# The opening of a fused attention and expert kernel, written as some 680 jobs of one engine each

## The chip, the cores and the metric

The kernel runs on one core of a Trainium2 chip. The metric is device time in microseconds (us) of one execution. The engines are PE (matrix products, with PEld for its weight loads), DVE (vector), ACT (scalar functions), POOL (GpSimd) and SP (which here only issues transfers). A row of PE that is one pass of a matrix product is called a matmul below.

## What is computed

```python
rel = pos[:, None] - pos[None, :]
mask = (rel >= 0) & (rel < 64)
scores = np.where(mask, scale * q @ k.T, -1e9)     # batch 8, heads 8, 576 tokens, 64 wide
attn = softmax(scores) @ v
x = attn.transpose(0, 2, 1, 3).reshape(4608, 512)
xn = x / rms(x) * rms_g
g = xn @ w_gate                                    # 512 x 1536
out = (g * sigmoid(g) * (xn @ w_val)) @ w_out      # 1536 x 512
```

So it is attention over a sliding window of 64 keys, a normalisation of each token's 512 numbers, and an expert network of three weight matrices.

## The kernel before

**Precision.** Each product of the expert network is made of 16-bit halves: an operand is a high and a low f16 part, and `three` (L1008) adds high*high, high*low and low*high, so a line L1009, L1010 and L1011 stand for one product. The weights come in a wide format and are first turned into such halves on the chip. For one chunk (256 of the 1536 hidden columns, gate or val) that is: a transfer of 1 MB by `stage` (L222), two exponentials on ACT and two pairs of `pw` matmuls on PE with a DVE operation behind each (`widen_powers`, `widen_rest`), a maximum on DVE, a common scale (`in_scale`: one small matmul and a few small DVE and POOL operations), and the split (L261 to L269): high half on ACT, low half on DVE or POOL.

**Stages.** The opening, up to 230 us, works on three things at once:
- Attention of batches 0 and 1, four pairs of heads each. A pair has two groups. A group is `scores` (64x64 matmuls of line L433 into two PSUM banks, one for each head of the pair), masks on DVE (L446), exponentials on ACT (L449), the sums' reciprocals on DVE, a scaling on POOL (L533), transposes on PE (`tr`, L548), copies by DVE and ACT (L551), the products with the values on PE (`xp`, L597) and a copy into `xb`. After four pairs come the sums of squares: `tot` on PE (L852), eleven small DVE operations for the inverse roots (L868 to L875), a broadcast on PE (`rb`, L921), and the normalised token halves `xn` on DVE, ACT and POOL (L950 to L959).
- The preparation of the six chunks of gate and val, and of the six of `w_out`.
- The first tile of 512 tokens: for each of 12 blocks of 128 hidden columns the matmuls `pg` and `pv` (12 each), tanh on ACT, two DVE operations, the hidden halves; then `po`, four token blocks of 36 matmuls each. The second tile has its first two chunks (EARLY = 2) here too.

Tile 1's third chunk (`pg_1_4`) and all that comes behind it is called the tail below. There the remaining batches, tiles and weights are woven into one written order.

**What sets the order.** In the tail, each instruction is tied to the one written ahead of it on its engine ("written order", at the end of the program). In the opening the program only emits its parts in an order: hand-set numbers (`CFG['X']`, `['DW']`, `['DO']`, `S1`, `SC0`, `N0` and others) say at which half step of the expert work (`tick`, `advance`) which part is emitted, `behind` adds hints, and a scheduler that models the engines then chooses the order of each queue. `scores` emits its matmuls with the heads taking turns:

```python
QUARTERS = ((0, 0), (1, 1), (0, 1), (1, 0))      # head, half of the bank's rows
for i in range(2):
    for h, par in QUARTERS:
        quarter(sc[h][par * D : (par + 1) * D, i, :], qt, kk, h, 4 * g + 2 * i + 1 + par)
```

The banks of PSUM in the opening are: three `mo` (products of the expert network, and the scores of batch 0), two `xp` (also `pw`), and one each of `sc`, `tr` and `mi`. The scores of batch 1 take `sc` for one head and `mi` for the other; `mi` also serves `n2`, `tot` and `rb`.

Of the kernel before, what the change touches and what calls it, by code (L numbers as in the profile page):

```python
CFG = {'X': {'p00': 6.0, 'b00': 8.44, 't00': 9.52, 'p01': 8.44, 'b01': 10.94, 't01': 10.94, 'r': 2, 'z0': 11.94, 's00': 15.12, 's01': 12.94, 'p10': 18.61, 'd10': 8, 'd11': 13.94}, 'DW': {'d10': -6, 'p10': -4, 'b10': -12, 't10': -4, 'd11': -4, 'p11': -2.0, 'b11': -2, 't11': -1.98, 'z1': 2, 's10': 2.1, 's11': 2.05, 'd20': -2, 'p20': 0, 'b20': 0.01, 't20': 0.02, 'd21': 0, 'p21': 2, 'b21': 2, 't21': 2.02, 'z2': 6, 's20': 6, 's21': 6.05, 'd30': 2, 'p30': 2.0, 'b30': 4, 't30': 4.02, 'd31': 4, 'p31': 6, 'b31': 6.01, 't31': 8, 'z3': 10, 's30': 10.1, 's31': 11.96, 'd40': 6, 'p40': 7, 'b40': 8, 't40': 8.02, 'd41': 5.69, 'p41': 10, 'b41': 10.01, 't41': 12, 'z4': 14, 's40': 14.1, 's41': 14, 'd50': 10, 'p50': 12, 'b50': 12, 't50': 12.02, 'd51': 12, 'p51': 13.49, 'b51': 14, 't51': 14, 'z5': 15.0, 's50': 18, 's51': 18, 'D0': 17, 'W0': 19, 'D1': 18.66, 'W1': 21.59, 'D2': 19.5, 'W2': 21.5, 'D3': 20.5, 'W3': 22, 'D4': 21.5, 'W4': 22.5, 'D5': 22, 'W5': 23.5, 'O': 24.5}, 'LO': '0000100010101000', 'ADD': 'ppvppp', 'ONP': '000001110101', 'ONO': '000000', 'FB': 1, 'NB0': 0, 'HIE': 'aaaaavaaaaaa', 'HOE': 'aaaaaa', 'HHE': 'aavaaaaavaaaaaaaavavaaaa', 'XHE': 'aavvvaaaaavvaava', 'XBE': 'aaaaavaaaaaavaaa', 'X2E': 'aaaaavaa', 'DO': 'q0 k0 q1 v0 k1 q2 k2 v1 q3 k3 v2 s0 v3 s1'}

# [24 lines left out]
P = 128  # L27
# [15 lines left out]
LT0 = [1.62, 1.62, 1.62, 1.62, 1.76, 1.62, 1.76, 1.62]  # L43
LV0 = [2.6, 2.6, 2.6, 2.6, 2.6, 2.6, 2.6, 2.6]
# [37 lines left out]
def tile_window_attention_moe(  # L82
# [10 lines left out]
    nc = tc.nc  # L93

    cp = ctx.enter_context(tc.tile_pool(name="cp", bufs=1))
    wk = ctx.enter_context(tc.tile_pool(name="wk", bufs=2))
    early = ExitStack()
    ps_sc = early.enter_context(tc.tile_pool(name="ps_sc", bufs=1, space=PSUM))
    ps_tr = early.enter_context(tc.tile_pool(name="ps_tr", bufs=1, space=PSUM))
    ps_x = early.enter_context(tc.tile_pool(name="ps_x", bufs=2, space=PSUM))  # L100
    ps_mi = early.enter_context(tc.tile_pool(name="ps_mi", bufs=1, space=PSUM))
    ps_mo = early.enter_context(tc.tile_pool(name="ps_mo", bufs=3, space=PSUM))
# [15 lines left out]
    pt_pool = early.enter_context(tc.tile_pool(name="pt", bufs=NPT))  # L118
# [71 lines left out]

    def exp_bits(dst, src):
        nc.vector.tensor_scalar(dst, src.bitcast(I32), 23, None, ALU.logical_shift_right)
# [11 lines left out]
    def rms_weights():  # L204

        nc.sync.dma_start(out=gsb, in_=rms_g)
        nc.vector.tensor_reduce(gmx[:, 0:1], gsb, AX.X, ALU.max, apply_absolute_value=True)
        gps = ps_mi.tile([P, TT], F32, tag="mi", name="gps")
        nc.tensor.transpose(gps[0:1, 0:P], gmx[:, 0:1], ident)
        nc.vector.tensor_reduce(gmx[0:1, 1:2], gps[0:1, 0:P], AX.X, ALU.max)  # L210
        nc.vector.tensor_tensor(gmx[0:1, 1:2], gmx[0:1, 1:2], floor[0:1, :], ALU.max)
        gpb = ps_mi.tile([P, TT], F32, tag="mi", name="gpb")
        nc.tensor.matmul(gpb[:, 0:1], lhsT=one[0:1, :].to_broadcast([1, P]), rhs=gmx[0:1, 1:2], start=True, stop=True)
        exp_bits(gex[:, 0:1], gpb[:, 0:1])
        nc.vector.tensor_scalar(gex[:, 1:2], gex[:, 0:1], 1.0, None, ALU.add)
        nc.vector.tensor_scalar(gex[:, 2:3], gex[:, 0:1], -1.0, 253.0, ALU.mult, ALU.add)
        pow2(gpw, gex[:, 1:3])
        nc.vector.tensor_scalar(gsb, gsb, gpw[:, 1:2], None, ALU.mult)
        nc.vector.tensor_scalar(gsb_late, gsb, -0.1875, None, ALU.mult)


# [9 lines left out]
    def widen_powers(st, name):  # L231

        n = 1024
        by = st.bitcast(U8)
        top = by[:, 8 : 8 + 8 * n].rearrange("p (i e) -> p i e", e=8)[:, :, 0]
        mp = wk.tile([P, n], BF16, tag="t2k", name=f"mp_{name}", bufs=T2K)
        mn = wk.tile([P, n], BF16, tag="t2k", name=f"mn_{name}", bufs=T2K)
        nc.scalar.activation(mp, top.bitcast(I8), AF.Exp, bias=ebias[:, 0:1], scale=LN2_16)
        nc.scalar.activation(mn, top, AF.Exp, bias=ebias[:, 1:2], scale=LN2_16)
        return mp, mn  # L240

    def widen_rest(st, dst, mp, mn, name):

        for i in range(2):
            cols = slice(i * TT, (i + 1) * TT)
            pw = x_bank(f"pw_{name}_{i}")
            nc.tensor.matmul(pw, lhsT=unit[:, 0, :], rhs=mp[:, cols], start=True, stop=False)
            nc.tensor.matmul(pw, lhsT=unit[:, 1, :], rhs=mn[:, cols], start=False, stop=True)
            rest = st[:, 1 + 2 * i * TT : 1 + 2 * (i + 1) * TT].rearrange("p (i e) -> p i e", e=2)[:, :, 0]
            nc.vector.scalar_tensor_tensor(  # L250
                dst[:, cols].bitcast(I32), rest, 5, pw.bitcast(I32), ALU.logical_shift_right, ALU.bitwise_or
            )

    def widen(st, dst, name):
        mp, mn = widen_powers(st, name)
        widen_rest(st, dst, mp, mn, name)
        return mp

    def split(src, sc, hi, lo, on_pool, hv):
        if on_pool:  # L260
            nc.vector.tensor_scalar(src, src, sc, None, ALU.mult)  # L261
            (nc.vector.tensor_copy if hv else nc.scalar.copy)(hi, src)
            nc.gpsimd.tensor_tensor(lo, src, hi, ALU.subtract)
            return
        if hv:
            nc.vector.tensor_scalar(hi, src, sc, None, ALU.mult)
        else:
            nc.scalar.activation(hi, src, AF.Copy, scale=sc)
        nc.vector.scalar_tensor_tensor(lo, src, sc, hi, ALU.mult, ALU.subtract)  # L269

    def in_stage(c, i):
        w = (w_gate, w_val)[i]
        return stage(w[:, c * WC : (c + 1) * WC], NKD, f"{i}_{c}")

    tops = {}
    staged = {}
# [41 lines left out]
    def out_stage(c):  # L318
        return stage(w_out[c * WC : (c + 1) * WC, :], 2, f"o_{c}")
# [218 lines left out]
    def weights_to_keys(n, g, ps):  # L538
        pts = []
        for h in range(2):  # L540
# [11 lines left out]
            if g == h == 0:  # L552
                cpy(pt[0:D, 2, :], tr[0:D, 2, :])
# [1084 lines left out]
```

## Time and profile before

| | before |
|---|---|
| median of 3 runs | 962.68 us |
| lowest, highest | 959.09, 964.14 us |
| profiled execution | 962.36 us |
| its span | 960.6 us |
| PE busy | 934.6 us, 97% |
| DVE, ACT, POOL busy | 72%, 58%, 43% |
| mean granted clock of TensorE | 0.988 |

The span goes from the first to the last instruction of the profiled execution; 1.76 us lie around it. A row of the timeline gives start, duration, engine, line, operation, tiles, shape and count, and in brackets the idle time ahead of it with what ended it. Durations of merged rows reach from the first start to the last end; matmuls overlap, so a row of matmuls in a stream costs less than its duration says: the 512-column matmul is shown with 0.38 us and the next starts 0.21 to 0.22 us later.

### The profile page before, as it was taken

To read this page: it belongs to the slowest core of one execution; us is meant where nothing else is said; L and a number is where in the kernel's file an instruction comes from. 1 tells how busy PE (TensorE), PEld (TensorE's weight loads), DVE (VectorE), ACT (ScalarE), POOL (GpSimd) and SP (SyncE) were. 2 spreads that over 40 slices of the span, in tenths; PEclk is the share of its full clock that TensorE was granted. 3 is DMA by queue.
4 is the path that set the end of the run, shared out by engine and by line. 5 is a ranking of instruction groups with operands and counts; after the bars stand their busy time and mean duration, and the time that the engine had idled before them with its cause. 6 is when DMAs were issued, how large, how long until landed. Compare 5 with 4: busy or idle time off the path is not lost.

```text
span 960.6 us, 22333 instructions
## 1 busy us (share of the span) xinstructions
PE 934.6 (97%) x8350; PEld 683.6 (71%) x8363; DVE 689.0 (72%) x1868; ACT 558.4 (58%) x1434; POOL 413.4 (43%) x477
## 2 busy tenths in 40 slices
PE   7889999999999999999999999999999999999998
PEld 5654554444444444477888888888888888888887
DVE  5679675763778676989977887888788876733770
ACT  6658677743435553657666756775676545533552
POOL 3335562241515362445734563555454544430540
PEclk9979999899999999999999999999999999999999
DMA  8555453052736766489749974987497646555641
GB/s 306 164 158 173 139 184 132 13 158 68 177 91 175 220 194 202 147 255 319 226 179 302 315 244 154 321 281 254 154 316 265 204 144 223 172 175 196 212 154 45
DMA packets 102812, 187.59 MB, mean 195 GB/s; under 512 B 27440, under 2 KB 64304, under 8 KB 102704
## 3 DMA queue, kind: packets, MB, share of 16 engines
q1 hardware_dynamic: 102128, 184.98, 60.0%
q8 instruction: 66, 1.08, 0.5%
q10 hardware_dynamic: 576, 1.18, 0.3%
q14 instruction: 42, 0.34, 0.1%
HBM read 148.38 MB, written 37.75 MB: 194 GB/s over the span
## 4 chain that ended last, share of the span: by engine, by line
PE 86%; DVE 8%; ACT 2%; issue 2%; DMA 1%; POOL 1%; SPq 0%; DVEq 0%; ACTq 0%; POOLq 0%
PE a L1262 30%; PE o L1205 17%; PE sc L433 4%; PE pg L1009 3%; PE pg L1010 3%; PE pv L1009 3%; PE pg L1011 3%; PE pv L1011 3%; PE pv L1010 3%; PE x L571 3%; PE po L1009 2%; PE po L1011 2%; PE po L1010 2%; PE xp L597 1%; PE tr L548 1%
## 5 line engine op out<-in xcount | busy, mean ns | idle before, releaser
L1262 PEld LDWEIGHTS <-wt 128*128 128x128 f16 x3024 | 294.0, 98 | 39.1 <-issue 3.5
L1262 PE MATMUL a<-xn,wt 128*128 128x256 f16 x1728 | 203.9, 273 | 2.3 <-DVE th L1292 2.0
L1331 POOL TENSOR_TENSOR wt<-u,wt 128x512 f16<-128x512 f32 x72 | 65.8, 914 | 169.1 <-ACT wt L1329 111.8
L1262 PE MATMUL a<-wt,wt 128*128 128x256 f16 x1044 | 126.4, 273 | 0.0
L1296 ACT ACTIVATE th<-a,hsc 128x256 f32<-128x256 f32 x144 | 68.1, 473 | 99.3 <-DVE a L1360 85.3
L1331 POOL TENSOR_TENSOR h<-th,h 128x512 f16<-128x512 f32 x72 | 84.1, 1170 | 48.9 <-ACT h L1329 48.5
L1205 PE MATMUL o<-wt,h 128*128 128x256 f16 x864 | 100.4, 273 | 0.0
L1205 PEld LDWEIGHTS <-h 128*128 128x128 f16 x864 | 84.1, 98 | 10.7 <-issue 1.0
L449 ACT ACTIVATE pm<-pm,st 128x128 f32<-128x128 f32 (+1 forms) x216 | 83.9, 390 | 10.5 <-DVE st L446 9.6
L1360 DVE TENSOR_TENSOR a<-a,s 128x512 f32<-128x512 f32 x72 | 50.0, 695 | 48.2 <-PE a L1262 45.7
L404 POOL TENSOR_TENSOR pm<-pm,st 128x512 f32<-128x512 f32 (+1 forms) x72 | 63.0, 901 | 30.9 <-DMA kv<-kv 22.5
L1291 DVE SCALAR_TENSOR_TENSOR th<-th,a 128x256 f32<-128x256 f32 x144 | 59.6, 414 | 20.4 <-ACT th L1296 18.5
L1062 POOL TENSOR_TENSOR h<-th,h 128x512 f16<-128x512 f32 x30 | 36.7, 1224 | 80.4 <-ACT h L1061 68.4
L1205 PEld LDWEIGHTS <-wt 128*128 128x128 f16 x648 | 63.4, 98 | 8.9 <-issue 1.4
L433 PE MATMUL sc<-kv,q 64*64 64x128 f32 (+1 forms) x1056 | 60.3, 299 | 9.2 <-DMA q<-q 4.8
L1292 DVE SCALAR_TENSOR_TENSOR th<-a,th 128x256 f32<-128x256 f32 x144 | 61.1, 424 | 4.9
L433 PEld LDWEIGHTS sc<-kv,q 64*64 64x64 f32 x1056 | 46.0, 147 | 20.8 <-issue 6.3
L1009 PE MATMUL pg<-xn,wt 128*128 128x512 f16 x144 | 55.8, 387 | 1.1 <-ACT ot L1456 0.8
L1009 PE MATMUL pv<-xn,wt 128*128 128x512 f16 x144 | 55.4, 385 | 0.3 <-issue 0.2
L1010 PE MATMUL pg<-xn,wt 128*128 128x512 f16 x144 | 55.3, 384 | 0.1
L1010 PE MATMUL pv<-xn,wt 128*128 128x512 f16 x144 | 54.9, 381 | 0.1
L1011 PE MATMUL pv<-xn,wt 128*128 128x512 f16 x144 | 54.9, 381 | 0.1
(218 smaller groups left out, 1938.6 us busy)
## 6 DMA issues: line engine op xcount, KB each, us to landing
wt<-sevens SPq DMA_DIRECT2D x72, 512.0 KB, 5.2
wt<-sevens SPq DMA_DIRECT2D x36, 768.0 KB, 5.2
wt<-outer SPq DMA_DIRECT2D x24, 768.0 KB, 5.8
kv<-kv SPq DMA_DIRECT2D x28, 608.0 KB, 5.5
via<-pm SPq DMA_DIRECT2D x96, 144.0 KB, 3.3
pm<-via SPq DMA_DIRECT2D x24, 576.0 KB, 4.6
q<-q SPq DMA_DIRECT2D x28, 288.0 KB, 3.9
st<-w_gate SPq DMA_DIRECT2D x6, 1024.0 KB, 5.5
```

The lines of the kernel that those rows point to most:

```text
L404: nc.gpsimd.tensor_tensor(p[:, :ks, us, :], p[:, :ks, us, :], r, ALU.mult)
L433: nc.tensor.matmul(out.rearrange("p (n c) -> p n c", c=D), lhsT=qt[hd, j * D : (j + 1) * D], rhs=halves[hd, :1, :] if j == 0 else halves[h ...
L449: nc.scalar.activation(part, part, AF.Exp, bias=low, scale=-1.0, accum_out=total)
L1009: nc.tensor.matmul(acc, lhsT=lh, rhs=rh, start=first, stop=False)
L1010: nc.tensor.matmul(acc, lhsT=lh, rhs=rl, start=False, stop=False)
L1011: nc.tensor.matmul(acc, lhsT=ll, rhs=rh, start=False, stop=last)
L1205: nc.tensor.matmul(acc[:, sub * HT : (sub + 1) * HT], lhsT=l[:, x, sub * P : (sub + 1) * P], rhs=r[:, y, :], start=first and c == cs[0] an ...
L1262: nc.tensor.matmul(acc[:, i * HT : (i + 1) * HT], lhsT=ws[l][:, kt, :], rhs=b[:, m, kt, :], start=at_start, stop=kt == 1 and j == 2, skip_ ...
L1291: nc.vector.scalar_tensor_tensor(cols, cols, 1.0, acc[:, :HT], ALU.add, ALU.mult)
L1292: nc.vector.scalar_tensor_tensor(cols, acc[:, HT:], 2.0**-42, cols, ALU.mult, ALU.mult)
L1296: nc.scalar.activation(cols, acc[:, :HT], AF.Tanh, scale=th_scale[:, c : c + 1])
L1331: nc.gpsimd.tensor_tensor(lo, src, hi, ALU.subtract)
```

## The change

The functions that emitted parts of the opening (`scores`, `weights_to_keys`, `attention_events`, `first_batch`, `widen_rest`, `in_scale`, `expert_in`, `expert_out`, `tick`, `advance`, `behind` and others) give way to functions that declare jobs. A job has a name, a part that issues instructions of one engine, the jobs that it needs, and the buffers that it takes, each with the job that gives it back. `run_jobs` calls the parts in the order of a table of numbers, `ORDER`; a job whose needs are not met lets a later one by that stands at most `AHEAD` behind it. The place of `mark`, from which instructions are tied into written order on all five queues, moves ahead of the first job.

```diff
+ORDER = {'g0': 7.16, 'g1': 1.88, 'g2': 11.07, ..., 's41': 60.66, 'm410': 185.07, ..., 'V1': 200.24}
+AHEAD = 3.0
+IDLES = 0
+NUDGE = {}
...
+    def run_jobs(steps):
+        late = max(ORDER.values(), default=0)
...
+        def next_of(left):
+            limit = ORDER.get(left[0], late) + AHEAD
+            for n in left:
+                if ORDER.get(n, late) > limit:
+                    break
+                if not needs(n):
+                    return n
+            return first_of(left[0], set()) or next(n for n in left if not needs(n))
...
-    def scores(n, g, qk):
+    def group_jobs(n, g, box, norm):
...
+        tags = [("mo", f"m{k}1"), ("mo", f"m{k}1")] if n < NPAIR else [("sc", f"m{k}1"), ("mi", f"m{k}1")]
+        job(f"s{k}", score, f"q{n}", f"k{n}", takes=tags)
         for h in range(2):
+            job(f"m{k}{h}", partial(mask, h), f"s{k}", *([f"m{k}0"] if h else []),
+                takes=[] if h else [("st", f"w{k}1"), ("t2k", f"t{k}0"), ("t2k", f"t{k}1")])
+            job(f"a{k}{h}", partial(power, h), f"m{k}{h}")
+            job(f"w{k}{h}", partial(scaled, h), f"i{k}")
+            job(f"t{k}{h}", partial(turned, h), f"w{k}{h}", takes=[("sc" if n < NPAIR and h else "tr", f"u{k}{h}")])
...
-    def expert_in(t, c):
+    def expert_jobs(t, c):
...
+            for m in range(2):
+                job(f"G{k}{m}", partial(products, i, m), f"l{c}{m}", *xs, *([f"G{t}{c}00"] if i or m else ["v61"] if t else []),
+                    takes=where + [("mo", f"{'MN'[m]}{k}")])
...
-    rest = first_batch()
-    rest(1)
...
     mark = traced[-1]
+    rms_jobs()
+    for b in range(TB):
+        batch_jobs(b)
+    for c in range(NC):
+        in_jobs(c)
+    out_jobs()
+    idle_jobs(IDLES)
+    for t, cs in ((0, NC), (1, EARLY)):
+        for c in range(cs):
+            expert_jobs(t, c)
+    out_tile_jobs(0)
+    run_jobs([f"G{t}{c}{i}{m}" for t, cs in ((0, NC), (1, EARLY)) for c in range(cs) for i in range(2) for m in range(2)]
+             + [f"U{k}{half}" for k in range(TT // P) for half in range(2)])
     rest_of_tiles()
```

The instructions are the same ones but for a square of batch 1 (128x576), which moves from DVE to ACT. From `pg_1_4` on, the queues hold what they held. So the change is in the order of the opening on all queues. Three places of PE's queue show it. The names are tile names with the pair of heads or the tile first; a count behind a row is that of equal rows on end.

The first place is a score group of batch 1 (pair 6, group 0; the third number of the name is the head). Before, a head's five matmuls stand together, and the other head's come some 80 rows later:

```order
L433 MATMUL sc_6_0_0_1133<-kv_6_766,q_6_764 64x128 x4
L433 MATMUL sc_6_0_0_1133<-kv_6_766,q_6_764 64x64
L433 MATMUL sc_6_0_1_1134<-kv_6_766,q_6_764 64x128 x4
L433 MATMUL sc_6_0_1_1134<-kv_6_766,q_6_764 64x64
```

Now:

```order
L549 MATMUL sc_6_0_0_994<-kv_6_735,q_6_688 64x128
L549 MATMUL sc_6_0_1_995<-kv_6_735,q_6_688 64x128
L549 MATMUL sc_6_0_0_994<-kv_6_735,q_6_688 64x128
L549 MATMUL sc_6_0_1_995<-kv_6_735,q_6_688 64x128
L549 MATMUL sc_6_0_0_994<-kv_6_735,q_6_688 64x128
L549 MATMUL sc_6_0_1_995<-kv_6_735,q_6_688 64x128
L549 MATMUL sc_6_0_0_994<-kv_6_735,q_6_688 64x128
L549 MATMUL sc_6_0_1_995<-kv_6_735,q_6_688 64x128
L549 MATMUL sc_6_0_0_994<-kv_6_735,q_6_688 64x64
L549 MATMUL sc_6_0_1_995<-kv_6_735,q_6_688 64x64
```

The heads take turns, as the program emits them, and the group is one block. So it is in all 19 groups of pairs 0 to 10 in the change; before, in the very first and in pair 10.

The second place is that from the sums of batch 0 to the first expert product (`pw_0_1` and `pw_1_1` belong to chunk 1 of gate and of val). Before:

```order
L852 MATMUL tot_0_639<-one_94,ssq_0_296 128x1 x5
L921 MATMUL rb_0_0_660<-ident_86,rm_0_645 128x128 x4
L433 MATMUL sc_4_0_0_703<-kv_4_691,q_4_689 64x128 x4
L433 MATMUL sc_4_0_0_703<-kv_4_691,q_4_689 64x64
L1009 MATMUL pg_0_0_824<-xn_0_659,wt0_81 128x512
L1009 MATMUL pv_0_0_837<-xn_0_659,wt0_81 128x512
```

Now, with every second row of like ones left out:

```order
L979 MATMUL tot_0_646<-one_94,ssq_0_474 128x1 x5
L1051 MATMUL rb_0_0_666<-ident_86,rm_0_652 128x128 x4
L350 MATMUL pw_0_1_0_677<-mp_0_1_673,unit_91 128x512
L350 MATMUL pw_0_1_0_677<-mn_0_1_675,unit_91 128x512
L350 MATMUL pw_0_1_1_680<-mp_0_1_673,unit_91 128x512
L350 MATMUL pw_0_1_1_680<-mn_0_1_675,unit_91 128x512
L549 MATMUL sc_4_0_0_694<-kv_4_357,q_4_538 64x128
L549 MATMUL sc_4_0_1_695<-kv_4_357,q_4_538 64x128
L350 MATMUL pw_1_1_1_711<-mp_1_1_686,unit_91 128x512
L350 MATMUL pw_1_1_1_711<-mn_1_1_708,unit_91 128x512
L549 MATMUL sc_4_1_1_750<-kv_4_357,q_4_538 64x128
L1162 MATMUL pg_0_0_767<-xn_0_665,wt0_81 128x512
```

Eight `pw` matmuls and both groups of pair 4 have moved ahead of the first product; behind it, `pg_0_0` has its twelve matmuls on end where they were mixed with `pv_0_0` and `pg_0_1`. On DVE the two low halves of chunk 0 now both stand between the roots and the four operations of L1075 (L950 before), which are followed by the bits of `pw_0_1`, one cast of `xn` and the six masks of `sc_4_0`.

The third place is around the broadcast of batch 1, between tile 0 and tile 1. Before, from the last matmul of tile 0's hidden blocks on, one row of each kind:

```order
L1011 MATMUL pv_0_11_1866<-xn_0_659,wt2_83 128x512
L433 MATMUL sc_8_1_1929<-kv_8_1634,q_8_1632 64x128 x6
L921 MATMUL rb_1_0_1773<-ident_86,rm_1_1715 128x128 x3
L921 MATMUL rb_1_0_1773<-ident_86,rm_1_1715 128x64
L433 MATMUL sc_9_0_2034<-kv_9_1758,q_9_1824 64x128 x8
L433 MATMUL sc_9_1_2035<-kv_9_1758,q_9_1824 64x128 x8
L1009 MATMUL pg_1_0_1914<-xn_1_749,wt0_81 128x512
```

Now, the same way:

```order
L1164 MATMUL pg_0_10_1720<-xn_0_665,wt2_83 128x512
L979 MATMUL tot_1_1741<-one_94,ssq_1_1103 128x1 x5
L1164 MATMUL pv_0_11_1770<-xn_0_665,wt2_83 128x512
L1051 MATMUL rb_1_0_1788<-ident_86,rm_1_1747 128x128 x3
L1051 MATMUL rb_1_0_1788<-ident_86,rm_1_1747 128x64
L1162 MATMUL pv_0_10_1808<-xn_0_665,wt2_83 128x512
L1164 MATMUL pv_0_10_1808<-xn_0_665,wt2_83 128x512
L1162 MATMUL pg_1_0_1873<-xn_1_802,wt0_81 128x512
```

The blocks `pv_0_11` (the rest of it), `pv_0_10` and `pg_0_11` have moved to either side of the broadcast, and pairs 8 and 9 from ahead of `pg_1_0` to behind it.

## Rows read from the trace of the kernel before

**Rows 1.** The page: busy time of each engine, and the chain that ended last.
```profile
PE 934.6 (97%) x8350; PEld 683.6 (71%) x8363; DVE 689.0 (72%) x1868; ACT 558.4 (58%) x1434; POOL 413.4 (43%) x477
...
PE 86%; DVE 8%; ACT 2%; issue 2%; DMA 1%; POOL 1%; SPq 0%; DVEq 0%; ACTq 0%; POOLq 0%
```

**Rows 2.** Timeline of PE, where tile 0 ends and tile 1 goes on.
```profile
228.97 0.38 PE L1011 MATMUL po<-wt,h 128*128 128x512 f16 x1
230.13 0.38 PE L1009 MATMUL pg<-xn,wt 128*128 128x512 f16 x1 [0.78 <-ACT ot L1456]
```

**Rows 3.** Windows of 50 us: length, busy us (instructions) of each engine, PEclk, DMA share, GB/s.
```profile
0.00:50.00 50.00, 40.20 (x345) 29.74 (x347) 29.86 (x149) 30.33 (x99) 18.29 (x39) 0.98 0.69 238
50.00:100.00 50.00, 45.60 (x294) 24.79 (x300) 42.56 (x133) 35.40 (x82) 21.19 (x30) 0.89 0.52 162
100.00:150.00 50.00, 49.79 (x364) 26.72 (x365) 33.10 (x82) 37.56 (x69) 29.41 (x31) 1.00 0.42 141
```

**Rows 4.** What PE waited for up to 230 us: us in total, times, longest.
```profile
PE sc L433 <- DVE st L446: 3.6, 4, 2.1
```

**Rows 5.** Timeline of PE: score groups of batches 0 and 1.
```profile
4.85 2.18 PE L433 MATMUL sc<-kv,q 64*64 64x128 f32 x28 [4.85 <-DMA q<-q]
...
35.04 1.12 PE L433 MATMUL sc<-kv,q 64*64 64x128 f32 x8
...
67.73 0.76 PE L433 MATMUL sc<-kv,q 64*64 64x128 f32 x10
```

**Rows 6.** Timeline of PE: a score group of a later batch, and what follows it.
```profile
235.40 0.27 PE L433 MATMUL s<-kv,q 64*64 64x64 f32 x2
...
236.35 1.24 PE L571 MATMUL x<-pm,kv 64*64 64x128 f32 x36
```

**Rows 7.** Windows of the score line L433 alone, columns as in rows 3.
```profile
0.00:48.00 48.00, 15.63 (x144) 1.00 0.68 235
48.00:150.00 102.00, 13.07 (x160) 0.94 0.48 154
150.00:172.00 22.00, 5.64 (x48) 0.89 0.43 144
```

**Rows 8.** Timeline of PE: the same two transposes on either side of 40 us.
```profile
36.09 0.69 PE L548 MATMUL tr<-ident,p 128*128 128x128 f32 x2
...
42.37 0.44 PE L548 MATMUL tr<-ident,p 128*128 128x128 f32 x2
```

**Rows 9.** Timeline of PE: from the sums of batch 0 to the first expert product.
```profile
47.24 2.06 PE L852 MATMUL tot<-one,ssq 128*128 128x1 f32 x10 [1.41 <-DVE ssq L719]
51.68 2.04 PE L921 MATMUL rb<-ident,rm 128*128 128x128 f32 x8 [2.38 <-DVE rm L875]
...
55.22 0.58 PE L1009 MATMUL pg<-xn,wt 128*128 128x512 f16 x1 [0.23 <-ACT xn L957]
```

**Rows 10.** Timeline of DVE behind the roots of batch 0.
```profile
51.45 1.28 DVE L269 SCALAR_TENSOR_TENSOR wt<-wt,ws 128x1024 f16<-128x1024 f32 x1
53.76 2.72 DVE L950 SCALAR_TENSOR_TENSOR xb<-xb,gsb,rb 128x512 f32<-128x512 f32 x4 [1.04 <-PE rb L921]
56.40 1.74 DVE L957 CAST xn<-xb 128x512 f16<-128x512 f32 x2
```

**Rows 11.** Line L446, the masks, up to 230 us: ns min/median/max.
```profile
L446 DVE DVE_READ_ACCUMULATOR2_ANT st<- x107: 73/82/85, 7.4 to 213.7; 128x1 f32 x91, 64x1 f32 x16
L446 DVE CUSTOM_DVE_ANT_0 p<-sc,blocked x80: 209/285/293, 7.2 to 121.4; 128x128 f32<-128x128 f32 x64, 64x64 f32<-64x64 f32 x16
```

**Rows 12.** Timeline of PE: from the last product of tile 0 to the first of tile 1.
```profile
159.95 0.38 PE L1011 MATMUL pv<-xn,wt 128*128 128x512 f16 x1
...
166.93 1.94 PE L433 MATMUL sc<-kv,q 64*64 64x128 f32 x16 [2.11 <-DVE st L446]
...
171.67 0.61 PE L1009 MATMUL pg<-xn,wt 128*128 128x512 f16 x1
```

**Rows 13.** Line L269, the low halves, up to 230 us: ns min/median/max.
```profile
L269 DVE SCALAR_TENSOR_TENSOR wt<-wt,hsc x3: 1277/2082/2205, 184.5 to 194.7; 128x1024 f16<-128x1024 f32 x3
```

More of the change, by code (lines that the diff above doesn't have):

```diff
@@ L189, in tile_window_attention_moe, with job, idle_jobs, idle @@
     out_scale = hsc[:, 4, 0:1]
+    jobs = {}
+    def job(name, part, *after, takes=()):
+        assert name not in jobs, name
+        jobs[name] = part, list(after), list(takes)
+    SIZES = {"t2k": T2K, "st8": NST, "pt": NPT, "st": 3, "mo": 3, "sc": 1, "tr": 1, "mi": 1, "xp": 2, "kv": NKV, "q": NQ, "f4k": F4K,
+             "xn": 2, "xb": 1, "ssq": 1, "top": 2, "n2": 2, "z": 2, "ws": 2, "rm": 1, "mo1": 1}
+    spare = {}
+    def idle_jobs(count):
+        def idle(k):
+            if k == 0:
+                spare["to"] = ps_tr.tile([P, TT], F32, tag="tr", name="idle")
+            nc.tensor.matmul(spare["to"][:, 3 * P :], lhsT=ones, rhs=ones, start=True, stop=True, skip_group_check=True)
+        for k in range(count):
+            job(f"Y{k}", partial(idle, k), *(["Y0"] if k else []), takes=[] if k else [("tr", None)])
@@ L229, in stage, with widen_jobs @@
         return st
-    def widen_powers(st, name):
+    def widen_jobs(name, tiles, load, dst, free):
+        box = {}
         n = 1024
[L234 to L240, printed above, removed]
@@ new lines, in product, with rest @@
+        def product(j):
+            dst()
+            box["pw", j] = ps_x.tile([P, TT], F32, tag="xp", name=f"pw_{tiles}_{j}")
+            for i in range(2):
+                nc.tensor.matmul(box["pw", j], lhsT=unit[:, i, :], rhs=box[i][:, j * TT : (j + 1) * TT], start=i == 0, stop=i == 1)
+        def rest(j):
+            bits = box["st"][:, 1 + 2 * j * TT : 1 + 2 * (j + 1) * TT].rearrange("p (i e) -> p i e", e=2)[:, :, 0]
+            nc.vector.scalar_tensor_tensor(
+                dst()[:, j * TT : (j + 1) * TT].bitcast(I32), bits, 5, box["pw", j].bitcast(I32), ALU.logical_shift_right, ALU.bitwise_or
+            )
@@ new lines, in begin @@
+        def begin():
+            box["st"] = load()
+        job(f"d{name}", begin, takes=[("st8", f"r{name}1")])
+        for i in range(2):
+            job(f"e{name}{i}", partial(power, i), f"d{name}", takes=[("t2k", f"f{name}" if free and i == 0 else f"p{name}1")])
+        for j in range(2):
+            job(f"p{name}{j}", partial(product, j), f"e{name}0", f"e{name}1", takes=[("xp", f"r{name}{j}")])
+            job(f"r{name}{j}", partial(rest, j), f"p{name}{j}")
+        if free:
+            job(f"f{name}", lambda: free(box[0]), f"r{name}0", f"r{name}1")
@@ L512, in scores @@
             for i, u in enumerate(units(g, h)):
                 part[u] = p[:, i, :]
[L514 to L518 removed]
+                low = own["st"][:, 0, u - u0 : u - u0 + 1]
                 if u:
@@ L721, in roots @@
-        def roots():
-            assert chain["add", b] == NPAIR
-            norm["r"] = inverse_roots(b, norm["ssq"])
+                else:
+                    nc.gpsimd.tensor_tensor(ssq, ssq, pairs[hp][0], ALU.add)
         def wide_parts(piece):
             return wide_roots(b, norm["ssq"], pairs[NPAIR - 1][0], piece)
-        def normal(piece):
-            for part in normalise(b, norm["x"], norm["r"], piece):
-                part()
         def normal_parts(piece):
-            return normalise(b, norm["x"], norm.get("r"), piece)
```

781 lines of the change are left out of this document (410 added, 371 removed).

## The prediction

> **What bounds the kernel now.** I read the page first: PE is busy for 97% of the span and makes up 86% of the chain that ended last; no other engine is over 72% [rows 1]. So what counts is when PE gets through its queue. From `pg_1_4` on all queues hold the same rows in the same order, so the change can only move the moment at which that tail begins: 230.13 us, 1.16 us after the last `po` matmul [rows 2]. I take the tail as rigid: a microsecond won ahead of it is one won at the end. Work and waits in the opening are therefore the whole question.
>
> Next the windows: in the first 50 us PE is busy for 40.2, in the second for 45.6 at a granted clock of 0.89, in the third for 49.8 [rows 3]. Between 50 and 100 DVE has 42.6 us of work: it is the engine that comes next. Then the waits: PE's longest in the middle of the opening are for masks ahead of scores, 3.6 us in four, the longest 2.1 [rows 4], and 2.38 us for the roots of batch 0 [rows 9].
>
> Last the timeline, for what one kind of work costs in either order. The first group of scores, 20 matmuls with the heads in turns, and eight of the second group, head by head, take 2.18 us together; such eight alone take 1.12 [rows 5]. That leaves 1.06 for the 20, or 0.053 each; 1.12/8 is 0.14. In the tail, where heads take turns too, 36 matmuls take 236.35 - 235.40 = 0.95 us, 0.026 each [rows 6]; ten of one head in batch 1 take 0.76, 0.076 each [rows 5]. The factor of two between the early prices is the clock: two transposes take 0.69 us at 36 us and 0.44 at 42 [rows 8], so up to some 40 us PE runs at the lower level (1.2 GHz), though the clock's column shows nothing there. At either level the order of the heads is worth a factor of about 2.5.
>
> **The change part by part.**
>
> *A, the time up to `tot` of batch 0.* Scores there take 15.63 us for 144 matmuls [rows 7]; in turns 144 x 0.053 = 7.6, so PE has 8.0 us less to do. But PE also waits there: 4.85 us for the first queries [rows 5], 1.41 us ahead of `tot` [rows 9], some 10 us in all (50 - 40.2, rows 3), and DVE and ACT have 30 us each [rows 3] in chains of mask, exponential, reciprocal, scaling, transpose. Upper bound of the gain: 8.0 + 1.4 = 9.4. Lower bound: the 1.4 and no more, if these chains set the pace. I take 5.2, nearer the middle: `tot` starts at 42 and not at 47.24 us.
>
> *B, from `tot` to the first product.* Before: 55.22 - 47.24 = 8.0 us [rows 9]. Now PE's written order puts eight `pw` matmuls and both groups of pair 4 ahead of `pg_0_0`. The second head of the first of these groups takes the `mi` bank, which `rb` holds until L1075 has read it four times; the second group waits for the masks of the first. DVE's chain: `tot` to roots 4.2 us (51.45 - 47.24), two low halves of 1.28 where one stood, four operations of 2.72 [rows 10], two bit operations of about 0.7 (an estimate, from L950's 2.72/4 for the same 512 columns), a cast of 1.74/2, six masks of 0.285 + 0.082 [rows 11] (2.2, two of them smaller): 4.2 + 2.6 + 2.7 + 1.4 + 0.9 + 2.2 = 14. So `pg_0_0` starts 14 to 15 us behind `tot`, six later than before. PE isn't empty meanwhile. Before had 15 products done by 61.9, 14.6 us behind `tot` (rows 9 give the first; in a stream one starts every 0.216 us): 3.2 us of work; the change has five more `pw` (1.1) and 14 more score matmuls (0.4) done instead. Given back: 3.2 - 1.5 = 1.7, between 0 (if the bank comes free earlier) and 4 (if PE, with little to do for so long, also falls to the lower clock).
>
> *C, scores of batch 1 and of half of pair 8.* 13.07 us for 160 matmuls [rows 7]; in turns 160 x 0.026 = 4.2. Less work: 8.9. It counts as far as PE stays the bound. DVE has 42.6 + 33.1 = 75.7 us in these 100 [rows 3], which would be 83% of 91. In the slices with DVE at its full rate some of it goes to waits. I take 7.5, between 3 and 8.9.
>
> *D, between the tiles.* From the last product of tile 0 to the first of tile 1 PE takes 171.67 - 159.95 = 11.7 us, with 2.11 us of waiting for a mask and, behind it, 16 scores in 1.94 us, 0.12 each, which is the lower clock again [rows 12]. The work there at full rate: 48 scores in turns 1.3 (5.64 before, rows 7), `rb` 1.0 (half of rows 9's 2.04, which is at the lower level), ten `pw` of 0.216, a product: 4.7. Now 24 products and more stand around `tot` and `rb`, and pairs 8 and 9 come behind `pg_1_0`, so that roots, normalisation and masks have PE work beside them. Gain 7.0, at least the scores' 4.3, at most 8 with the first slow products.
>
> *E, new waits.* A strict order waits where a looser one would have had something else ready. Candidates are `pw_1_2`, whose transfer waits for a buffer, and the last splits of `w_out` ahead of `po`. The trace doesn't show them; the nearest rows are the waits for masks, 0.9 us on average [rows 4]. I allow two such, 2 us, between 0 and 6. The square that moves to ACT costs nothing: ACT has 37.6 of 50 us there [rows 3]; without that cover it would be under 1 us.
>
> Sum: -5.2 + 1.7 - 7.5 - 7.0 + 2 = **-16.0 us**. The profiled execution took 962.36, so 946.4; it lies 0.3 below the median of the runs, on which I forecast **947 us**.
>
> **The rivals.**
>
> *DVE becomes the bound.* With its work pressed into less time, DVE sets the pace between 57 and 135 us and its operations get longer. For it: the 42.6 of 50 us; the same low half took 1.28 us at one time and 2.08 to 2.21 at another [rows 13]. Against: half of the low halves would have to fall on such times. Seven of them at +0.8 are 5.6 us; with A at 3 and C at 3 instead of 5.2 and 7.5 the gain is 16 - 2.2 - 4.5 = 9, less a part of the 5.6: 5 to 9, **955 us**. The Trainium skill (SBUF — State Buffer, "Who interferes with whom") says that a DVE instruction with two inputs in SBUF and a GpSimd instruction that reads SBUF exclude each other for the whole of an instruction. The longer low halves fit that rule; no row of this trace shows which instruction held the port.
>
> [...]
>
> *Strict order blocks PE.* Scores in turns need both banks empty at once; head by head needed one. PE's queue stands at the first score until the masks of the group ahead are done, and so does everything behind it, products included. The price: at most the 2.1 us of rows 4 for each of 16 groups, 34 us, 978 in all. Without waits the gain is 18; the kernel gets slower by more than 4.8 us if the 16 cost over 1.4 us each. Against: the groups now stand some 25 products apart, longer than six masks take. If it goes so, **970 us**.
>
> *Nothing moves.* A at 1.4, B at 4, C at 3, D at 4.3, E at 5: about 0. Each opening order is then bound by the same chains of DVE and ACT: **962 us**.
>
> **How the numbers follow.** A measurement of this kernel can tell some 0.5%, 4.8 us, from no change: below 957.9 is faster, above 967.5 slower. My forecast (941 to 952) 0.58; early clock 0.10; DVE as the bound 0.13, nearly all of it below 957.9; nothing moves 0.11; blocked by strict order 0.08. Faster 0.58 + 0.10 + 0.13 = 0.81, same 0.11, slower 0.08. The range reaches from 938, with the early clock's better half, to 959, which takes in the DVE case and leaves out the last two.
>
> **What would show it.** In the profile after: `tot` of batch 0 near 42 us and `pg_0_0` near 57; score rows of 16 to 20 matmuls that take 0.026 to 0.053 us each; line L433's successor down from 34 to some 14 us; no stretch of 10 us between tiles with PE under 9; `pg_1_4` near 214 us; waits of scores for masks still under 5 us. I am wrong if `pg_1_4` starts after 225 us, if the scores wait for masks by more than 10 us in total, or if the tail, counted from `pg_1_4`, isn't as long as before.

## The result and the profile after

The changed kernel takes 934.64 us (median of 4 runs, 933.96 to 935.30) against 961.10 beside it (median of 4, 959.09 to 964.14): a ratio of 0.9722, 95% interval 0.9691 to 0.9754. The gain of 26.5 us has the forecast sign, but is ten more than the forecast 16 and lies outside the range. The profiled execution took 935.09 us, with a span of 933.3.

The page, busy times and chain [rows 1]:

```profile
PE 909.2 (97%) x8350; PEld 667.4 (72%) x8363; DVE 685.7 (73%) x1867; ACT 557.6 (60%) x1435; POOL 410.2 (44%) x477
...
PE 86%; DVE 5%; ACT 2%; DMA 2%; issue 2%; POOL 1%; SPq 0%; POOLq 0%; ACTq 0%; DVEq 0%
```

The shares are what they were; PE has 25.4 us less of busy time for the same number of matmuls. Where the tail begins, in PE's timeline [rows 2]:

```profile
202.86 0.38 PE L1164 MATMUL po<-wt,h 128*128 128x512 f16 x1
204.06 0.38 PE L1162 MATMUL pg<-xn,wt 128*128 128x512 f16 x1 [0.83 <-ACT ot L1641]
```

`pg_1_4` starts at 204.06 and not at 230.13 us, 26.1 earlier, and the same 1.2 us behind the last `po`. The span is 27.3 shorter, so the tail is rigid to within 1.2 us, as assumed. Windows of the opening [rows 3], columns as there, and one more of 50 us:

```profile
0.00:50.00 50.00, 35.29 (x379) 25.57 (x383) 36.98 (x172) 36.52 (x106) 18.88 (x39) 0.88 0.72 251
50.00:100.00 50.00, 49.64 (x414) 26.87 (x418) 44.12 (x145) 38.47 (x93) 24.69 (x36) 0.98 0.52 172
100.00:150.00 50.00, 49.66 (x314) 25.39 (x319) 37.22 (x90) 41.86 (x75) 26.68 (x29) 1.00 0.46 164
150.00:200.00 50.00, 49.22 (x322) 23.72 (x322) 30.39 (x93) 26.56 (x77) 15.52 (x17) 1.00 0.32 91
```

The second to fourth windows hold 49.6, 49.7 and 49.2 us of PE; only 1.5 of 150 us are lost. Before, the second had 45.6 at a clock of 0.89. DVE rose from 42.6 to 44.1 in the second window, and still isn't the bound. PE's timeline in batch 0 and behind it [rows 8, 9]:

```profile
16.48 0.69 PE L672 MATMUL tr<-ident,p 128*128 128x128 f32 x2
...
25.30 0.44 PE L672 MATMUL tr<-ident,p 128*128 128x128 f32 x2
...
37.23 0.38 PE L399 MATMUL n<-sq,one 128*128 128x2 f32 x2 [1.07 <-DVE sq L395]
38.28 2.13 PE L979 MATMUL tot<-one,ssq 128*128 128x1 f32 x10 [0.66 <-DVE z L403]
42.79 2.04 PE L1051 MATMUL rb<-ident,rm 128*128 128x128 f32 x8 [2.38 <-DVE rm L1005]
...
51.91 0.48 PE L1162 MATMUL pg<-xn,wt 128*128 128x512 f16 x1
```

Two transposes fall from 0.69 to 0.44 us between 16 and 25 us, where before this happened between 36 and 42: the higher level of the clock comes some 19 us sooner (the trace's first record of the clock stands at 21.4 us, and at 40.7 before; ahead of it the level is read from the transposes). The level falls again as `tot` starts, behind two waits of PE, and `tot` and `rb` cost 2.1 and 2.0 us as before. `tot` starts at 38.3 (before 47.2), `pg_0_0` at 51.9 (before 55.2), 13.6 us behind `tot`. All matmuls, and those of the score line alone, up to the start of the tail (columns: length, PE busy, PEclk, DMA share, GB/s):

```profile
0.00:204.06 204.06, 187.04 (x1438) 0.97 0.52 171
0.00:204.06 204.06, 20.75 (x396) 0.97 0.52 171
```

The same two rows of the kernel before:

```profile
0.00:230.13 230.13, 212.42 (x1439) 0.96 0.48 155
0.00:230.13 230.13, 36.21 (x396) 0.96 0.48 155
```

PE's idle time in the opening is 230.13 - 212.42 = 17.7 us before and 204.06 - 187.04 = 17.0 now. The gain is nearly all busy time: 25.4 us less of it, 15.5 in the score line and 9.9 in other matmuls, more of which ran at the higher level. In the opening before, the lower level held up to 40.7 us and from 47.5 to 57.8, 81.7 to 85.1 and 167.0 to 173.8, 61.2 us in all; in the change up to 21.4 and from 38.5 to 52.1, 35.0 us. Outside the scores PE was busy for 30.1 us at this level before and for 13.1 in the change; at half the clock the 17 us between them are some 8.5 us of added work (an estimate from these figures), most of the 9.9.

The same two rows up to `tot` of batch 0, first before, then in the change:

```profile
0.00:47.24 47.24, 38.14 (x335) 1.00 0.67 233
0.00:47.24 47.24, 15.63 (x144) 1.00 0.67 233
0.00:38.28 38.28, 26.83 (x336) 1.00 0.81 281
0.00:38.28 38.28, 9.71 (x144) 1.00 0.81 281
```

PE has 11.3 us less to do there, 5.9 in scores and 5.4 in others, and is idle for 11.5 us instead of 9.1; so `tot` comes 9.0 us sooner.

Between the tiles [rows 12] there is nothing left to see but `tot` and `rb` in a full stream:

```profile
131.71 1.17 PE L979 MATMUL tot<-one,ssq 128*128 128x1 f32 x10
...
136.19 1.00 PE L1051 MATMUL rb<-ident,rm 128*128 128x128 f32 x8
```

### The profile page after: what moved, and what is told of

Its sections match the earlier page's. It is cut to its first block, busy times and chain, and to the rows that moved or that the text cites. A ratio compares the mean times of both kernels' runs of the same rounds, so it can differ in the third digit from the quotient of the medians.

```text
span 933.3 us, 22320 instructions
## 1 busy us (share of the span) xinstructions
PE 909.2 (97%) x8350; PEld 667.4 (72%) x8363; DVE 685.7 (73%) x1867; ACT 557.6 (60%) x1435; POOL 410.2 (44%) x477
## 4 chain that ended last, share of the span: by engine, by line
PE 86%; DVE 5%; ACT 2%; DMA 2%; issue 2%; POOL 1%; SPq 0%; POOLq 0%; ACTq 0%; DVEq 0%
PE a L1447 32%; PE o L1390 18%; PE pg L1162 3%; PE sc L549 3%; PE pg L1163 3%; PE pg L1164 3%; PE pv L1162 3%; PE pv L1164 3%; PE pv L1163 3%; PE x L737 3%; PE po L1162 2%; PE po L1163 2%; PE po L1164 2%; PE tr L672 1%; PE pw L350 1%
## 5 line engine op out<-in xcount | busy, mean ns | idle before, releaser
L1447 PEld LDWEIGHTS <-wt 128*128 128x128 f16 x3024 | 293.9, 98 | 39.4 <-issue 3.8
L1516 POOL TENSOR_TENSOR h<-th,h 128x512 f16<-128x512 f32 x72 | 84.0, 1169 | 49.1 <-ACT h L1514 48.7
L1390 PEld LDWEIGHTS <-wt 128*128 128x128 f16 x648 | 63.4, 98 | 8.9 <-issue 1.4
L1162 PE MATMUL pg<-xn,wt 128*128 128x512 f16 x144 | 54.7, 380 | 1.1 <-ACT ot L1641 0.8
L1164 PE MATMUL pg<-xn,wt 128*128 128x512 f16 x144 | 54.6, 379 | 0.0
L1163 PE MATMUL pg<-xn,wt 128*128 128x512 f16 x144 | 54.6, 379 | 0.0
L1164 PEld LDWEIGHTS <-wt 128*128 128x128 f16 x296 | 29.0, 98 | 35.2 <-DVE wt L382 0.3
L1162 PEld LDWEIGHTS <-wt 128*128 128x128 f16 x296 | 29.4, 99 | 33.1 <-issue 0.8
```

The costliest lines, as they stand in the source:

```text
L1162: nc.tensor.matmul(acc, lhsT=lh, rhs=rh, start=first, stop=False)
L1163: nc.tensor.matmul(acc, lhsT=lh, rhs=rl, start=False, stop=False)
L1164: nc.tensor.matmul(acc, lhsT=ll, rhs=rh, start=False, stop=last)
L1390: nc.tensor.matmul(acc[:, sub * HT : (sub + 1) * HT], lhsT=l[:, x, sub * P : (sub + 1) * P], rhs=r[:, y, :], start=first and c == cs[0] an ...
L1447: nc.tensor.matmul(acc[:, i * HT : (i + 1) * HT], lhsT=ws[l][:, kt, :], rhs=b[:, m, kt, :], start=at_start, stop=kt == 1 and j == 2, skip_ ...
```

## The experiments

Eleven kernels were run. Where a ratio is given, it is to the kernel before, on the same chip. Differences to the change are between medians that were not taken side by side; the kernel before took 961.1 us beside the change and 961.0, 959.4 and 961.2 beside the three groups of experiments, so they hold to some 2 us.

**The turns of the heads, taken away and added.** Two kernels issue a group's matmuls head by head, in the same place of the queue, in batch 0 (`apart0`) and in batch 1 (`apart1`); one adds the turns to the kernel before.

```diff
-            for i in range(2):
-                for h, par in QUARTERS:
-                    quarter(...)
...
+            for hs_ in ((0,), (1,)) if n < NPAIR else ((0, 1),):     # apart1: n >= NPAIR
+                for i in range(2):
+                    for h, par in QUARTERS:
+                        if h in hs_:
+                            quarter(...)
...
```

> The changed kernel, with the scores of batch 0 alone head by head, in the same place of the queue. Theory C (the turns in batch 0 also decide when PE's clock rises, at 21.7 us now and 40 before): the rise moves past 30 us, tot of batch 0 past 44 us, time 941 to 945. Theory D (only their direct price counts, 4 to 8 us on PE, part of it in the shadow of DVE and ACT): the rise stays below 25 us, tot at 39 to 42, time 936 to 939.

> The changed kernel, with the scores of batch 1's four pairs alone head by head. From 52 us on PE is never idle in the changed kernel, so theory T says that their whole price comes back: 144 matmuls at 0.076 to 0.08 and not 0.027 to 0.03, 7 us, time 941 to 943. Theory O: under 2 us, since waits that the turns bring in go away again, time below 937.

Measured: 934.97 us for `apart0` (0.9742, 0.9715 to 0.9769) and 935.05 for `apart1` (0.9744, 0.9712 to 0.9777): no difference from the change. Groups of batch 1 in PE's timeline, first with turns, as changed, then head by head:

```profile
63.39 0.67 PE L549 MATMUL sc<-kv,q 64*64 64x128 f32 x16
...
68.23 0.77 PE L549 MATMUL sc<-kv,q 64*64 64x128 f32 x20
68.93 0.34 PE L693 MATMUL xp<-pt,wt 128*64 128x64 f32 x4
```

```profile
62.15 0.68 PE L549 MATMUL sc<-kv,q 64*64 64x128 f32 x16
...
66.99 1.04 PE L549 MATMUL sc<-kv,q 64*64 64x128 f32 x20
```

Sixteen matmuls take 0.67 or 0.68 us in either order; in the groups with four more, of 64x64, head by head takes 0.27 us longer. All scores up to the tail take 22.2 us in `apart1` and 20.8 in the change. So the turns, on which the prediction set its price, are worth 1.5 us of PE's work in batch 1, where theory T had 7, and nothing that the time shows; theory O's number holds. In `apart0` scores take 21.0 us, the clock rose at 19.0 us and `tot` started at 38.1, so theory C fell, and theory D's 936 to 939 was too much as well.

```diff
+        mine = [i for i in nc.cur_bb.bb.instructions[had:] if i.engine == nc.tensor.engine]
+        for one_, two_ in zip(mine, mine[1:]):
+            tc.add_manual_dep(two_, one_.name, ..., reason="turns")      # order only, no semaphore
```

> The kernel before, with one thing added: the matmuls of a score group are tied to each other in the order in which they are emitted, heads in turns. Theory T (the turns are what the change is worth, as less PE work): the scores' busy time falls from 34 to some 16 us, and the time to 943 to 948 us, most of the way to 934.6. Theory O (the order of everything else is worth most of it): the scores get cheaper but the groups wait for both banks, and the time stays at 955 us or above. My value: 947.

Measured: 961.17 us, 1.0003 (0.9985 to 1.0021). All matmuls and scores up to the tail, and the longest new wait:

```profile
0.00:227.92 227.92, 203.06 (x1440) 0.95 0.47 156
0.00:227.92 227.92, 29.45 (x396) 0.95 0.47 156
...
PE tot L859 <- DVE ssq L726: 3.4, 1, 3.4
```

Scores cost 7 us less than before (29.5 and not 36.2), PE is busy for 9.4 less in all, and idle for 24.9 instead of 17.7: most of the saving turned into waits, and the tail started only 2.2 us earlier. The scheduler still put other matmuls between those of a group. Theory O's time holds, and my value of 947 missed.

**The written order, taken away.** `loose` moves the place of `mark` back to where the tail begins.

> The changed kernel, jobs and table as they are, but the written order begins at the tail again, so that the scheduler sets the opening's queues. It splits the heads again in 13 of 19 groups and mixes the products of three accumulators. Theory T: about half of the scores' saving goes, 943 to 948 us. Theory W (it is the tie to the written order that matters, turns or not): 955 or above, as before. Theory J (the jobs' order is enough, and the scheduler keeps most of it): under 939.

Measured: 974.31 us, 1.0161 (1.0123 to 1.0200), 1.6% slower than the kernel before; its tail starts at 241.6. PE's longest waits behind that for the first queries:

```profile
PE pg L1162 <- ACT wt L381: 3.6, 1, 3.6
PE pw L350 <- ACT xb L706: 3.5, 1, 3.5
PE pg L1163 <- DVE xn L1083: 1.9, 1, 1.9
```

PE waits for weights, for copies and for `xn`, which in the table's order stood ready, and scores cost 33.0 us again; PE is idle for 28.5 us ahead of the tail, where the change has 17.0. Theory W holds: the jobs and the table without the tie cost 13 us against the kernel before.

**Halves apart.** In `split` the second head's matmuls are held back until the next job of PE has been issued, or until the group's first mask needs them.

```diff
+            half_of(0)
+            halves.append((f"m{k}", partial(half_of, 1)))
...
+            if halves and name[0] != "s" and any(i.engine == nc.tensor.engine for i in nc.cur_bb.bb.instructions[had:]):
+                halves.pop(0)[1]()
```

> The changed kernel, with the two heads' halves of a score group no longer in one block: where masks allow, the next job of PE (transposes, value products or pw) stands between them, in 10 of the 16 groups of batches 0 and 1, 7 of them in batch 1. Theory B (what a score costs depends on whether both halves stand in one block, since 8 alone took 0.59 us to the next row and 16 in a block 0.60; the turns inside a block are worth nothing): 7 x 0.6 to 0.7 = 4.2 to 4.9 us in batch 1 and up to 2 in batch 0, time 938.5 to 941.5. Theory P (PE's work in scores isn't what the gain came from): below 936.

Measured: 944.30 us, 0.9847 (0.9803 to 0.9892), some 9.7 more than the change. A split group of batch 1 in the timeline, and all matmuls and scores up to the tail:

```profile
64.44 0.76 PE L555 MATMUL sc<-kv,q 64*64 64x128 f32 x10
65.13 0.44 PE L682 MATMUL tr<-ident,p 128*128 128x128 f32 x2
65.50 0.76 PE L555 MATMUL sc<-kv,q 64*64 64x128 f32 x10
66.19 0.39 PE L1172 MATMUL pv<-xn,wt 128*128 128x512 f16 x1
```

```profile
0.00:213.25 213.25, 199.23 (x1451) 0.97 0.50 164
0.00:213.25 213.25, 30.18 (x396) 0.97 0.50 164
```

Ten matmuls of one head take 0.69 us to the next row, as much as twenty of both in a block (0.70, from 68.23 to 68.93 in the changed kernel, above). A half costs what a whole costs. Scores rise from 20.8 to 30.2 us, PE is idle for 14.0, less than in the change, and the tail starts 9.2 us later: 4.0 of it up to `tot`, where the clock also rose later (30.8 us), the rest behind it. This is theory B, some 3 us above its upper end: behind `tot` scores cost 4.9 us more than in the change, as it said, but ahead of `tot`, where much of the work is at the lower level, 4.5 and not up to 2.

**Blocks in the kernel before.** If a block is all that is needed, the kernel before should win from it too. Here each score group is a barrier for the order of PE alone.

```diff
+        for i in pe[block_at[0]:]:
+            if i.name != mine[0].name and i not in mine:
+                tc.add_manual_dep(mine[0], i.name, note, reason="block")
```

(and the same from a group's last matmul to what is emitted behind it; the group's own matmuls are tied in their emitted order, heads in turns).

> The kernel before, with each score group of batches 0 and 1 as one block on PE: all that is emitted ahead of it stays ahead, all that is emitted behind it stays behind; the scheduler still sets the rest. Theory B (the blocks as such carry the gain, whatever stands around them): scores of these batches at some 15 us instead of 28, and 945 to 951 us. Theory Q (the saving only reaches the end where the rest of the queues is arranged around the blocks; here PE waits instead, as it did with the tied turns): 957 or above.

Measured: 990.15 us, 1.0314 (1.0277 to 1.0350). PE's longest waits, and all matmuls and scores up to its tail:

```profile
PE tr L564 <- POOL p L549: 8.2, 3, 3.1
PE pw_o L247 <- ACT mp_o L238: 4.9, 3, 2.4
PE gps L209 <- DVE gmx L207: 4.8, 1, 4.8
```

```profile
0.00:257.25 257.25, 203.79 (x1439) 0.89 0.42 139
0.00:257.25 257.25, 24.10 (x396) 0.89 0.42 139
```

Scores are down to 24.1 us, PE's work by 8.6, and yet the tail starts 27 us later: PE is idle for 53.5 us, and the granted clock up there is 0.89 where the kernel before has 0.96. Theory Q holds, far beyond its number: blocks alone are not enough.

**Between the tiles.** `nofill` moves `pv_0_11`, `pv_0_10`, `pg_0_11` and four `pw` ahead of `tot` of batch 1; `half` moves only `pv_0_10` and `pg_0_11`, from behind `rb` to ahead of it.

```diff
+ORDER.update({'G0511': 146.0, 'G0501': 146.1, 'G0510': 146.2, 'S1': 159.5, 'R1': 159.4, 'H100': 160.5, ...})   # nofill
+ORDER.update({'G0511': 149.4, 'G0501': 149.45, 'G0510': 149.5, 'H100': 160.5, ...})                        # half
```

> The changed kernel, with the products pv_0_11, pv_0_10, pg_0_11 and the pw of chunks 1 and 3 of w_out moved ahead of tot of batch 1, so that only four pw and rb stand between tot and pg_1_0. Theory F (the gain between the tiles comes from these products standing beside the roots and the normalisation): PE waits for about 2.4 (roots) and 3 to 4 us (normalisation), and may fall to the lower clock: 5 to 8 us, time 940 to 943. Theory M (it came from the masks of pairs 8 and 9 no longer standing ahead of pg_1_0): under 2.5 us, below 937.

> The changed kernel, with pv_0_10 and pg_0_11 moved from behind rb of batch 1 to ahead of it: 36 products stand between tot and rb, so the roots are covered as before, but only four pw stand between rb and pg_1_0. The full uncovering cost 13.5 us. Theory N (the normalisation behind rb is what needs cover; the roots are 2.4 of it and the clock's falls follow the waits): PE waits 3 to 5 us for xn, with one fall of the clock, time 940 to 944. Theory R (the wait for the roots and the clock's falls behind it were most of it): under 938.

Measured: 948.11 us (0.9895, 0.9862 to 0.9928) and 947.23 (0.9864, 0.9824 to 0.9905), 13.5 and 12.6 more than the change. PE's timeline in `nofill`, then in `half`:

```profile
146.15 1.94 PE L1052 MATMUL rb<-ident,rm 128*128 128x128 f32 x8 [2.38 <-DVE rm L1006]
...
151.59 0.38 PE L1163 MATMUL pg<-xn,wt 128*128 128x512 f16 x1 [1.85 <-ACT xn L1079]
152.25 0.38 PE L1164 MATMUL pg<-xn,wt 128*128 128x512 f16 x1 [0.28 <-DVE xn L1084]
...
155.62 0.59 PE L1164 MATMUL pg<-xn,wt 128*128 128x512 f16 x1 [2.56 <-POOL xn L1084]
```

```profile
143.16 1.00 PE L1052 MATMUL rb<-ident,rm 128*128 128x128 f32 x8
...
150.87 0.59 PE L1163 MATMUL pg<-xn,wt 128*128 128x512 f16 x1 [5.84 <-ACT xn L1079]
...
154.90 0.58 PE L1164 MATMUL pg<-xn,wt 128*128 128x512 f16 x1 [1.93 <-POOL xn L1084]
```

In `nofill` PE waits 2.38 us for the roots and 1.85, 0.28 and 2.56 for pieces of `xn`, and `rb` (1.94 us) and the products fall to the lower level. In `half` the roots are covered and nothing is gained by it: PE waits 5.84 and 1.93 us for `xn`. So it is the normalisation that needs the 24 products behind `rb`. Theories F and N hold in what PE waits for, but F's 5 to 8 us and N's 940 to 944 us were too little. These are the prices of uncovering this stretch in the changed order, not what it gained over the kernel before, which had 48 scores there.

**Versions meant to be faster.** `warm2` gives PE matmuls on constants where it waits in batch 0, `early` puts `pg_0_0` right behind `rb`, `early3` a little later, behind the weights it needs.

```diff
+ORDER.update({'Y0': -150.0, ...})                     # warm2: 8 ahead of the scores, 4, 2 and 9 around tot
+ORDER.update({'F000': 43.05, 'H000': 43.06, 'L000': 43.07, ..., 'G0000': 43.08})      # early
+ORDER.update({'H000': 47.7, 'L000': 47.71, ..., 'G0000': 47.72, 's40': 47.73})        # early3
```

> The changed kernel with matmuls on constants added to PE: 8 ahead of the first scores, while PE waits for the queries, and 15 around tot of batch 0, where PE waits for DVE (4 ahead of n, 2 ahead of tot, 9 ahead of rb). Theory C (the lower clock from 38 to 52 us and up to 21 us costs time at the end): tot and rb at the higher level, 1.2 and 1.0 instead of 2.1 and 2.0 us, and the early rise some 3 us sooner; 931 to 933.5. Theory D (DVE's chain sets the first product, and PE's clock there lies in its shadow): within 1 us of 934.6. If the added matmuls delay tot: up to 936.

Measured: 934.57 us (0.9757, 0.9722 to 0.9792), the same as the change. PE's timeline:

```profile
37.82 1.28 PE L981 MATMUL tot<-one,ssq 128*128 128x1 f32 x10
...
41.48 1.13 PE L1053 MATMUL rb<-ident,rm 128*128 128x128 f32 x8 [0.26 <-DVE rm L1007]
...
46.49 0.76 PE L551 MATMUL sc<-kv,q 64*64 64x128 f32 x18 [2.67 <-DVE xb L1077]
...
50.43 0.40 PE L1164 MATMUL pg<-xn,wt 128*128 128x512 f16 x1
```

`tot` and `rb` now cost 1.28 and 1.13 us, but the second head of pair 4's first group waits 2.67 us for the four L1075 (here L1077) to leave the bank that `rb` held, and `pg_0_0` starts 12.6 us behind `tot` instead of 13.6. Even that microsecond need not be the added matmuls': without them it was 12.7 in `apart1` and 12.1 in `apart0`. DVE's chain sets that stretch, and the clock of PE there lies in its shadow: theory D.

> The changed kernel, with pg_0_0 right behind rb of batch 0, ahead of eight pw and pair 4, and on DVE and ACT the casts of xn right behind L1075. Theory G (the 13.6 us from tot to the first product are a loss that the table left in): pg_0_0 starts 10 us behind tot, and 2 to 3 us are won, 931.5 to 933. Theory H (what comes earlier here comes later in pair 4, whose masks then hold up its transposes): within 1 us of 934.6, or up to 3 us slower.

> The changed kernel, with pg_0_0 ahead of pair 4's scores, but behind three of the four pw of chunk 1 and behind both halves of chunk 0's weights, which is what pg_0_0 waited for (3.2 and 2.3 us) when it stood right behind rb. Theory G (the table left a gain here): 932 to 933.5. Theory H (what is gained by an earlier product is lost by pair 4's later masks): 934 to 937. If products waits again for weights or xn: 938 or above.

Measured: 943.15 us (0.9844, 0.9806 to 0.9882) and 941.16 (0.9807, 0.9779 to 0.9836), 8.5 and 6.5 more than the change. In `early`, PE's timeline:

```profile
47.77 0.61 PE L1163 MATMUL pg<-xn,wt 128*128 128x512 f16 x1 [3.20 <-ACT wt L382]
...
51.12 0.61 PE L1165 MATMUL pg<-xn,wt 128*128 128x512 f16 x1 [2.32 <-DVE wt L383]
```

The first product comes at 47.8, but it waits for both halves of its weights, which now stand behind casts on ACT and DVE. In `early3` it doesn't wait; there `pw` waits for the bits of the chunk ahead on DVE (L355), 4.0 us in two, and scores for masks, 2.4 in four. So theory G fell in both. Theory H had the sign, but at most 3 us of loss; beside the masks that it named, PE waits for weights in the one and for bits in the other. None of the three kernels beats the change.

## Why the prediction was right or wrong

**What bounds it** was right: PE's queue up to `pg_1_4`, and a rigid tail, 26.1 us at its start and 27.3 in the span.

**The step that failed** is the sum's list of what gets cheaper: it has scores and waits, and no term for PE's other matmuls but a few of D's. The prediction itself puts PE at the lower level up to some 40 us, but in A counts this only for scores; for the rest the early clock stands beside the sum, with a chance of 0.10. The runs show 9.9 us less busy time in the other matmuls, 5.4 of it up to `tot`, with 35.0 us of the opening at the lower level where there had been 61.2. Taken out of the 26.1, they leave 16.2 us, next to the forecast 16.0. That is luck: scores gave 15.5 of these, where the forecast has their line go down by 20 (34 to 14), and the 2 us of new waits that it allows did not come.

Not all of this clock is the kernel's doing. Up to `tot` of batch 0 the change, `half`, `early`, `apart1`, `nofill` and `early3` have the same queue of PE; the level rose at 21.0 to 21.6 us in the first three profiles and at 16.2 to 16.8 in the others. Executions of the kernel before whose mean granted clock was 0.993 or more took 958.7 us in the median (18 of them), those with 0.990 or less 961.8 (15); the profiled one, with 0.988, is of the latter kind.

**The price of the turns** was the wrong mechanism, and too high. I compared eight matmuls of one head, standing alone, with twenty and thirty-six of both in turns, and laid the difference to the turns. The runs show that it is the block: head by head inside a block cost nothing in time (`apart0`, `apart1`), halves apart cost 9.7 us in ten of sixteen groups (`split`). The term kept its sign because the change makes blocks and turns at once. The slip is in the first step: from a row of 28 I took away eight at the price of eight that stood alone, as if a price did not depend on the neighbours.

**A**, 5.2 forecast, was 9.0, near its upper bound of 9.4, but not out of its own terms: scores gave 5.9 us and not 8.0, the other matmuls 5.4, and idle time took 2.3 back. The higher level came at 21.4 and not at 40.7 us. The early clock, which the range's lower end rests on, has no price of its own in any run. What they show is this: in the six profiles with the same queue, a rise 5 us earlier goes with `tot` at 37.8 to 37.9 instead of 38.2 to 38.5 us; in `before_turns` the level first rose at 21.2 us, and `tot` came 3.1 us sooner than before; in `split` it rose at 30.8, and `tot` came 4.0 us later than in the change.

**B** was right in length: 14 to 15 us forecast, 13.6 measured, and by DVE's chain, as `warm2` showed.

**C, D and E** fell short together. From `tot` on I forecast a gain of 10.8 us and 17.1 came: 9.5 less work in scores, 4.5 less in other matmuls, 3.1 less idle time. Term E, 2 us of new waits, had the wrong sign: from the first product to the tail PE was idle for 2.3 us, where before it had been for 6.0, 2.25 of them between the tiles. I took DVE's load from the windows [rows 3], but made no term of the 4.4 us that PE lost in the second of them (1.9 of these ahead of the first product), nor of the lower level behind its clock of 0.89.

**D**, 7 us, can't be read off alone, as products moved across it; its cause was right. Without the products beside roots and normalisation 13.5 us come back, and 12.6 even with those beside the roots in place.

**The rivals.** DVE as the bound did not happen (44.1 us of 50, PE at 49.6). The rule that the Trainium skill gives for the port that DVE and GpSimd share (SBUF — State Buffer, "Who interferes with whom") was put beside it; no run here tests it. Strict order blocking PE did not happen in this table: scores waited for masks once, for 0.7 us. In `before_block` an order that is strict for PE alone did block it, for 53.5 us, but at transposes, `pw_o` and `gps` more than at scores.

**The range** failed because I cut it at half of one rival, as if the terms were independent. Their favourable bounds add up to 9.4 + 0 + 8.9 + 8 + 0 = 26.3, close to the 26.1 that came, though not out of the same parts. One cause moved several of them the same way: between the tiles the clock fell at 167.0 us before, 146.1 in `nofill` and 147.3 in `half`, beside waits of 2.1, 2.4 and 5.8 us; in the change, which waits for nothing there, it did not fall.

## What to carry to other kernels

A price per instruction from a merged row holds only with the neighbours that it had: compare what one block costs, alone and beside another, before laying a difference to the order inside it. Work saved on a queue that others feed comes out at the end only if the order of all queues keeps it fed: blocks of scores came with 26 us less in one order, and with 29 us more in another. Where part of a stretch runs at the lower clock, the sum needs a term for all of PE's work there, not only for the rows that the change names. Where terms share a cause (here, a wait that went and the fall of the clock beside it), their errors add up, and the range should reach to the sum of the bounds.

## What the runs showed of the hardware

I had not expected that 64x64 fp32 matmuls of one head and of the other take no more time together than alone: ten 0.69 us, twenty 0.70. Nor that the granted clock, with much the same busy time of PE in the first 20 us (13.7 us before, 12.7 in the change), would rise at 21 us in the one and at 40 in the other, and that the same queue of PE would show a rise anywhere from 16.2 to 21.6 us. In the changed kernel and in the variants that keep its written order it fell again around `tot` of batch 0, where PE waits for DVE, except in `warm2`: with the added matmuls it held past `rb` (until 47.1 us), and no time came of it. In `loose` it fell at 35.9 us, 12 us ahead of `tot`.
